# Half-row product groups in the opening of a fused Fourier-mixing and attention kernel, with 48 score-maximum tiles ahead and zero products before the first loads

## The chip, the cores and the metric

The kernel runs on one core of one Trainium2 chip. The metric is the device time of one execution in microseconds; the time before is the median of three runs. A profiled execution stands beside them; its trace gives all durations.

## The reference

```python
def reference(A_x, A_dft_seq_re, A_dft_seq_im, A_dft_hid_re, A_dft_hid_im, B_x, B_wqkv, B_wo, gate_w):
    x = A_x                                             # [1, 2048, 512], float32
    g = sigmoid((x * gate_w).sum(-1, keepdims=True))
    # Fourier mixing: hidden DFT, then sequence DFT, real part only
    re = x @ dft_hid_re.T
    im = x @ dft_hid_im.T
    a = dft_seq_re @ re - dft_seq_im @ im
    # attention: 32 heads of 16
    q, k, v = split_heads(x @ wqkv)
    b = merge_heads(softmax(q @ k.T * 16 ** -0.5) @ v) @ wo
    return g * a + (1 - g) * b
```

## The kernel before

Matrix products that need float32 accuracy are made from parts: a matrix is split into a high part in the reduced format `float32r` (a cast, `hi_lo`) and a low part (source minus high part), and a product is the sum of three: high by high, high by low, low by high (`mm3`). A chain over the hidden size of 512 therefore has 4 x 3 = 12 products of 128 rows by 512 columns into one PSUM bank. There are eight banks: `banks[0..6]` and `psD`.

The work goes in stages.

**Opening.** The inputs are loaded into a ring of six scratch tiles `raw` (`RAW`), split by ScalarE (high) and VectorE or GpSimd (low), and q and k are made for four blocks of 512 rows. q and k go to DRAM by their parts. The first product needs the first `wqkv` and `xa_t` blocks.

**v and imaginary rows.** For each of 16 blocks of 128 rows, a chain makes v (to the tile `vt`: ScalarE copies one half, VectorE the other); for each of 16 blocks another chain makes the imaginary part of the hidden DFT (`wch`, `wcl`), which ScalarE and VectorE split into a tile `hl` (two buffers) and SyncE's queue writes to DRAM (`b_d`). After `s` = 6, 8, 10, 12 a block of `wo` is split on ScalarE and GpSimd and a block of `w_hid` loaded; after the first four imaginary chains these become `wre`, the weights of the real part, whose low parts GpSimd makes. These chains take turns of three banks (`turn_of("s")`).

Between these chains, from the eighth on, stand *visits*: `visit(i)` makes two pairs of maximum tiles. A maximum tile (`a_tile`) is a product of 48 rows (16 rows of q and k, three combinations of parts) for one head, 128 queries and 512 keys; VectorE reduces it to the row maxima. A pair is the same tile for the two heads of a head pair, on rows 0 to 47 and 64 to 111. They take turns of four banks (`turn_of("a")`). `LEAD` = 44 pairs are made there, and `a_next` counts them. When the 32 pairs of one half of a head pair are done, `m_parts` (a reduction on VectorE, two small operations on GpSimd) and then `m_rows` (a transposition on VectorE, four small DMAs each on SyncE's and GpSimd's queues, `qs<-mt`) are queued in `deferred`; they put the negated maxima as two more rows beside q, so that the score product subtracts them. One entry is taken from `deferred` at each visit, or at the end of each segment later.

**Main stage.** From line 378 on, a `segment` interleaves on TensorE: half-row products (64 rows) of the real hidden DFT and the sequence DFT (`d`, into `psD`), beside a score or a maximum tile on the other half of the rows. ScalarE takes the exponential of each score tile (`pt`). A segment ends with 16 products of exponentials by v (`pv`). The patterns `FULL`, `THIN` and `NINE` fix the order; a segment has eight maximum tiles until their stream is used up, and the lead of this stream over the scores stays as the stage before left it. A planner (`bank`, `read_by`) picks the bank of each score and maximum tile by an estimate of when it is free. Loads and the final steps are due at fixed score units (`plan`). The second half of a `d` chain waits, by a dependency added by hand, for a reader of the segment before, so that both halves of the rows do not write one bank at the same time.

At the end of the sequence DFT `end_tiles` loads the output weights (`wo_hl`, four DMAs of 512 KB, line 462) and the attention rows over the no longer needed `xab` tiles, and the output projection follows.

Of the kernel before, what the change touches and what calls it, by code (L numbers as in the profile page):

```python
# [9 lines left out]
F32 = mybir.dt.float32  # L10
F32R = mybir.dt.float32r
AF = mybir.ActivationFunctionType
ALU = mybir.AluOpType
AX = mybir.AxisListType

P = 128
S = 2048
D = 512
# [3 lines left out]
KT = D // P  # L22
NT = S // P
UNITS = NP * 32
LEAD = 44
RAW = 6
PSUM = bass.MemoryType.PSUM
DRAM = bass.MemoryType.DRAM
# [3 lines left out]
def mix_kernel(ctx: ExitStack, tc: tile.TileContext, xa_t, xa, wqkv, w_hid, w_seq, wo, gate_w, out):  # L32
# [5 lines left out]
    nc = tc.nc  # L38
    ctx.enter_context(tc.manual_schedule())

    banks = [ctx.enter_context(tc.tile_pool(name=f"ps{i}", bufs=1, space=PSUM)) for i in range(7)]
    psD = ctx.enter_context(tc.tile_pool(name="psD", bufs=1, space=PSUM))
# [6 lines left out]
    b_d = [dram.tile([P, 2, D], F32, name=f"b{s}") for s in range(NT)]  # L49
# [22 lines left out]
    xab = [const.tile([P, 4, 2, D], F32R, name=f"xab{tb}", tag=f"xab{tb}") for tb in range(4)]  # L72

    turns = dict.fromkeys("fsa", 0)

    def turn_of(kind):

        group = {"f": range(7), "s": range(3), "a": range(3, 7)}[kind]
        turns[kind] += 1
        return banks[group[(turns[kind] - 1) % len(group)]].tile([P, 512], F32, name="t")  # L80

    def hi_lo(hi, lo, src, lo_eng=None):
        nc.scalar.copy(hi, src)  # L83
        (lo_eng or nc.vector).tensor_tensor(lo, src, hi.bitcast(F32), ALU.subtract)  # L84

    def mm3(ps, sh, sl, mh, ml, first, last):
        nc.tensor.matmul(ps, sh, mh, start=first, stop=False)  # L87
        nc.tensor.matmul(ps, sh, ml, start=False, stop=False)  # L88
        nc.tensor.matmul(ps, sl, mh, start=False, stop=last)  # L89

    right = tc.tile_pool(name="st1", bufs=1, side="right", reuse_waits="tile")
    st1 = right.__enter__()
    wv = [[const.tile([P, D], F32R, name=f"wv{v}{kt}", tag=f"w{4 * v + kt}") for kt in range(KT)] for v in range(2)]
    wch = st1.tile([P, KT, D], F32R, name="wch")
    wcl = st1.tile([P, KT, D], F32R, name="wcl")
# [10 lines left out]
    def add(hi, lo, src, lo_eng, shape=None):  # L106
        todo.append((hi, lo, src, lo_eng, shape))
# [6 lines left out]
    def split(n):  # L114

        for _ in range(n):
            load_ahead()
            if loaded:
                hi, lo, raw, lo_eng, shape = loaded.pop(0)
                hi_lo(hi, lo, raw.rearrange("p (s t) -> p s t", s=4) if shape else raw, lo_eng)  # L120
            load_ahead()

    def add_x(tb, kt):
        x = xab[tb][:, :, :, kt * P:(kt + 1) * P]
        add(x[:, :, 0], x[:, :, 1], xa_t[tb, :, kt], nc.vector, True)


    with tc.tile_pool(name="qk", bufs=1, reuse_waits="tile") as pool:
        wh = pool.tile([P, 2, KT, D], F32R, name="wh")
        wl = pool.tile([P, 2, KT, D], F32R, name="wl")  # L130

        def mm_qk(ps, c, ct, tb, kt):
            cols = slice(ct * P, (ct + 1) * P)
            x = xab[tb][:, :, :, kt * P:(kt + 1) * P]
            mm3(ps, wh[:, c, kt, cols], wl[:, c, kt, cols], x[:, :, 0], x[:, :, 1], kt == 0, kt == KT - 1)

        def evac_qk(ps, c, ct, tb):
            hl = pool.tile([P, 2, D], F32R, name="hl", bufs=7)
            hi_lo(hl[:, 0], hl[:, 1], ps)
            nc.sync.dma_start(qk_d[c][:, ct * P:(ct + 1) * P, tb * 512:(tb + 1) * 512].rearrange("v p t -> p v t"),  # L140
                              hl.bitcast(F32))

        for kt in range(KT):
            add(wh[:, 0, kt], wl[:, 0, kt], wqkv[0, :, kt], nc.vector)
            add_x(0, kt)
        for kt in range(KT):
            add(wh[:, 1, kt], wl[:, 1, kt], wqkv[1, :, kt], nc.vector)
        for tb in range(1, 4):
            for kt in range(KT):
                add_x(tb, kt)  # L150
        for kt in range(KT):
            add(wv[0][kt], wv[1][kt], wqkv[2, :, kt], nc.gpsimd)
        for kt in range(KT):
            add(wch[:, kt], wcl[:, kt], w_hid[1, :, kt], nc.gpsimd)
        split(8)

        xgs = {}

        def gate_row(s):

            xg = xgs.pop(s)
            nc.vector.scalar_tensor_tensor(xg, xg, 1.0, gwb, op0=ALU.mult, op1=ALU.mult, accum_out=z[:, s:s + 1])
            if s + 5 < NT:
                xgs[s + 5] = staged(xa[s + 5])

        for tb in range(4):
            if tb == 2:
                assert not todo and not loaded
                nc.sync.dma_start(gwb, gate_w.broadcast_to([P, D]))
                xgs.update({s: staged(xa[s]) for s in range(5)})  # L170
            for c in range(2):
                if tb == 0 and c == 0:
                    pss = [turn_of("f") for _ in range(4)]
                    for kt in range(KT):
                        for ct in range(4):
                            mm_qk(pss[ct], c, ct, tb, kt)
                    split(4)
                    for ct in range(4):
                        evac_qk(pss[ct], c, ct, tb)
                    continue  # L180
                for ct in range(4):
                    ps = turn_of("f")
                    for kt in range(KT):
                        mm_qk(ps, c, ct, tb, kt)
                    split(1 if ct % 2 and tb else 2)
                    evac_qk(ps, c, ct, tb)
                    if tb > 1:
                        gate_row(8 * (tb - 2) + 4 * c + ct)
# [19 lines left out]
    deferred = []  # L208
    a_left = {}

    def a_tile(i, h, ps=None):
        p, j = divmod(i, 64)
        qt, kb = divmod(j, 4)
        if ps is None:
            ps = turn_of("a")
        r = slice(64 * h, 64 * h + 48)
        nc.tensor.matmul(ps, qs[p % 2][r, qt * P:(qt + 1) * P], ks[p % 2][r, kb * 512:(kb + 1) * 512],  # L217
                         start=True, stop=True)
        user = nc.vector.tensor_reduce(mx[p % 2][:, h, qt, kb:kb + 1], ps, AX.X, ALU.max)  # L219
        hf = j // 32  # L220
        a_left[p, hf] = a_left.get((p, hf), 64) - 1
        if not a_left[p, hf]:
            deferred.extend((partial(m_parts, p, hf), partial(m_rows, p, hf)))
        return user
# [32 lines left out]
    wrs = []  # L257
    a_next = 0

    def visit(i):  # L260

        nonlocal a_next
        if deferred:
            deferred.pop(0)()
        if i < 7 or a_next == LEAD:
            return
        for j in range(2):
            for h in range(2):
                a_tile(a_next, h)
            a_next += 1  # L270

    for s in range(NT):
        t = xab[s // 4][:, s % 4]
        ps = turn_of("s")
        for kt in range(KT):
            r = slice(kt * P, (kt + 1) * P)
            mm3(ps, t[:, 0, r], t[:, 1, r], wv[0][kt], wv[1][kt], kt == 0, kt == KT - 1)
        visit(s)
        pv = ps.rearrange("p (r h d) -> p r h d", h=2, d=DH)
        nc.scalar.copy(vt[:, s, :, 0:16], pv[:, :, 0])  # L280
        nc.vector.tensor_copy(vt[:, s, :, 17:33], pv[:, :, 1])
        if s in range(6, 14, 2):
            kt = (s - 6) // 2
            wt = st1.tile([P, 2, D], F32R, name="hl", bufs=2)
            hi_lo(wt[:, 0], wt[:, 1], wos.pop(0), nc.gpsimd)
            nc.sync.dma_start(wo_d[kt], wt.bitcast(F32))
            wrs.append(staged(w_hid[0, :, kt]))

    def spare(i, dt, name):

        return const.tile([P, 4, P], dt, name=name, tag=f"w{i}")


    wre = [[const.tile([P, D], F32R, name=f"wre{v}{kt}", tag=f"w{4 * v + kt}") for kt in range(KT)] for v in range(2)]
    ab = [xab[s // 4][:, s % 4] for s in range(NT)]
    for s in range(NT):
        t = ab[s]
        ps = turn_of("s")
        for kt in range(KT):
            r = slice(kt * P, (kt + 1) * P)  # L300
            mm3(ps, t[:, 0, r], t[:, 1, r], wch[:, kt], wcl[:, kt], kt == 0, kt == KT - 1)
        visit(NT + s)
        bt = st1.tile([P, 2, D], F32R, name="hl", bufs=2)
        hi_lo(bt[:, 0], bt[:, 1], ps)
        nc.sync.dma_start(b_d[s], bt.bitcast(F32))
        if s < KT:
            hi_lo(wre[0][s], wre[1][s], wrs.pop(0), nc.gpsimd)
    run_deferred()
    assert a_next == LEAD
    right.__exit__(None, None, None)  # L310
# [516 lines left out]
    users, valued = [], 0  # L827
# [80 lines left out]
    users = []  # L908
# [68 lines left out]
```

## Time and profile before

| | |
|---|---|
| median of 3 runs | 1710.47 us (1710.4 to 1710.5) |
| profiled execution | 1713.87 us |
| its span, first to last instruction | 1712.1 us |
| mean granted TensorE clock | 0.997 |
| busy: TensorE / VectorE / ScalarE / GpSimd | 99% / 80% / 73% / 42% |

Times are from the start of the span. A timeline row gives the start, the time from there to the end of the row's last instruction, the engine, the line, the operation, output and inputs, the shape, the count, and in brackets the idle time before it with what ended it. PE is TensorE's products, PEld its weight loads, DVE VectorE, ACT ScalarE, POOL GpSimd, SPq SyncE's queue. A product's row is as long as its passage through the array; products follow each other more closely than that, so the start of one to the start of the next is its cost. A row of a group of instructions gives the busy time, the mean of one in ns, and the idle time before them.

### The profile page before, as it was taken

Reading aid. Unit: us, or ns where it says so; the run is one execution under the profiler, and the core shown is the slowest. Engines: PE = TensorE matmul, PEld = TensorE weight load, DVE = VectorE, ACT = ScalarE, POOL = GpSimd, SP = SyncE. Lnnn points to the kernel's source line nnn. Section 1 sums busy time; section 2 is a strip of 40 time slices with the busy share of each in tenths; the row PEclk is TensorE's granted clock in tenths of the full one; section 3 lists DMA queues with packets and bytes.
Section 4 is the critical chain, followed back from the end, with each engine's and each line's share of the span. In section 5 each row is a group of like instructions: output and inputs, shape, how many; then the busy total and the mean of one; then the engine's idle time right before and its main releaser. Section 6 shows DMA issues by size and latency. Waiting matters only on the chain.

```text
span 1712.1 us, 33831 instructions
## 1 busy us (share of the span) xinstructions
PE 1693.7 (99%) x12731; PEld 1081.6 (63%) x12731; DVE 1376.3 (80%) x2298; ACT 1247.9 (73%) x2472; POOL 715.4 (42%) x775
## 2 busy tenths in 40 slices
PE   8999999999999999999999999999999999999997
PEld 7876666666666666666666666666666656555543
DVE  5448788888888888888888888888888888799943
ACT  5212288887787788778788788778778778778785
POOL 0211144454444455444444555545455555322230
PEclk9999999999999999999999999999999999999999
DMA  8972511314141525232146635241322535560114
GB/s 280 341 173 98 159 16 19 46 32 81 53 80 46 95 89 103 60 67 59 40 92 247 125 94 108 57 87 51 72 73 66 106 100 101 183 151 8 39 27 136
DMA packets 82484, 165.12 MB, mean 96 GB/s; under 512 B 19776, under 2 KB 20032, under 8 KB 78480
## 3 DMA queue, kind: packets, MB, share of 16 engines
q1 hardware_dynamic: 77968, 162.56, 37.1%
q8 instruction: 100, 1.64, 0.4%
q0 software_dynamic: 4352, 0.39, 0.3%
q14 instruction: 64, 0.52, 0.1%
HBM read 107.73 MB, written 54.52 MB: 95 GB/s over the span
## 4 chain that ended last, share of the span: by engine, by line
PE 97%; DVE 1%; DMA 1%; issue 0%; POOL 0%; ACT 0%; SPq 0%; DVEq 0%; POOLq 0%; ACTq 0%
PE d L378 38%; PE t L718 27%; PE t L217 11%; PE t L682 9%; PE t L87 4%; PE t L88 3%; PE t L89 3%; PE t L699 1%; DVE mx L219 1%; PE t L378 0%; DMA qs<-mt 0%; DMA raw<-wqkv 0%; DVE yp L559 0%; PE t L637 0%; DMA o<-osum 0%
## 5 line engine op out<-in xcount | busy, mean ns | idle before, releaser
L219 DVE TENSOR_REDUCE mx<-t 128x1 f32<-128x512 f32 x2048 | 1267.4, 682 | 218.2 <-PE t L217 185.0
L683 ACT ACTIVATE pt<-t 128x512 f32<-128x512 f32 x2048 | 1034.9, 632 | 14.4 <-PE t L682 10.5
L682 PE MATMUL t<-qs,ks 50*128 50x512 f32 x2048 | 745.0, 414 | 3.6 <-DMA qs<-mt 2.4
L217 PE MATMUL t<-ks,qs 48*128 48x512 f32 x2048 | 695.5, 404 | 0.3 <-DVE mx L219 0.2
L378 PE MATMUL d<-xab,ch 64*128 64x512 f32 x2016 | 648.6, 396 | 0.0
L718 PE MATMUL t<-pt,vt 128*32 128x512 f32 x3968 | 478.9, 600 | 0.0
L378 PEld LDWEIGHTS d<-xab,ch 64*128 64x128 f32 x2016 | 367.1, 185 | 131.7 <-issue 90.7
L217 PEld LDWEIGHTS t<-ks,qs 48*128 48x128 f32 x2048 | 366.4, 186 | 79.0 <-DVE mx L219 26.3
L378 PE MATMUL d<-xab,cl 64*128 64x512 f32 x1008 | 399.4, 396 | 0.0
L682 PEld LDWEIGHTS t<-qs,ks 50*128 50x128 f32 x2048 | 367.6, 185 | 39.4 <-ACT pt L683 12.6
L733 POOL TENSOR_TENSOR osum<-osum,oe 128x512 f32<-128x512 f32 x217 | 278.9, 1285 | 124.4 <-ACT oe L727 118.5
L727 ACT COPY oe<-t 128x512 f32<-128x512 f32 x217 | 127.3, 587 | 254.1 <-PE t L718 252.5
L718 PEld LDWEIGHTS t<-pt,vt 128*32 128x32 f32 x3968 | 105.1, 109 | 230.2 <-issue 149.9
L333 POOL CAST ch<-craw 128x512 fp32r<-128x512 f32 x126 | 77.0, 611 | 377.9 <-PE t L682 364.5
L378 PEld LDWEIGHTS d<-xab,cl 64*128 64x128 f32 x1008 | 186.2, 185 | 67.5 <-issue 53.6
L334 POOL TENSOR_TENSOR cl<-craw,ch 128x512 fp32r<-128x512 f32 x126 | 162.1, 1286 | 10.2
L240 POOL DMA_DIRECT2D qs<-mt x128 | 72.0, 568 | 101.5 <-DVE mt L236 94.6
L83 ACT CAST hl<-t 128x512 fp32r<-128x512 f32 x48 | 28.1, 586 | 85.2 <-PE t L89 67.3
L378 PE MATMUL d<-wre,xab 64*128 64x512 f32 (+1 forms) x348 | 85.5, 391 | 0.1
L378 PE MATMUL d<-wo_hl,o_hl 64*128 64x512 f32 (+1 forms) x261 | 69.7, 393 | 0.0
L378 PEld LDWEIGHTS d<-wre,xab 64*128 64x128 f32 (+1 forms) x348 | 64.0, 185 | 7.0 <-issue 1.1
L84 DVE TENSOR_TENSOR hl<-t,hl 128x512 fp32r<-128x512 f32 x48 | 32.9, 687 | 37.6 <-ACT hl L83 37.6
(115 smaller groups left out, 890.8 us busy)
## 6 DMA issues: line engine op xcount, KB each, us to landing
craw<-w_seq SPq DMA_DIRECT2D x128, 256.0 KB
qk<-hl SPq DMA_DIRECT2D x32, 512.0 KB
qs<-qk SPq DMA_DIRECT2D x96, 128.0 KB
ks<-qk SPq DMA_DIRECT2D x96, 128.0 KB
b<-hl SPq DMA_DIRECT2D x16, 512.0 KB
xab<-b SPq DMA_DIRECT2D x16, 512.0 KB
o<-osum SPq DMA_DIRECT2D x62, 128.0 KB
oh<-nh SPq DMA_DIRECT2D x12, 512.0 KB
```

Of the source, the lines that this page charges most:

```text
L87: nc.tensor.matmul(ps, sh, mh, start=first, stop=False)
L217: nc.tensor.matmul(ps, qs[p % 2][r, qt * P:(qt + 1) * P], ks[p % 2][r, kb * 512:(kb + 1) * 512], start=True, stop=True)
L219: user = nc.vector.tensor_reduce(mx[p % 2][:, h, qt, kb:kb + 1], ps, AX.X, ALU.max)
L240: (nc.sync, nc.gpsimd)[h].dma_start(rows.rearrange("v (q b c) -> v b q c", q=8, b=4)[:, b], mt[hf][32 * b + h:32 * b + 32:2])
L333: nc.gpsimd.tensor_copy(h1, raw)
L334: nc.gpsimd.tensor_tensor(l1, raw, h1.bitcast(F32), ALU.subtract)
L378: i = nc.tensor.matmul(self.ps, st[r], mv[r], start=not self.begun, stop=stop)
L682: nc.tensor.matmul(ps, ks[p % 2][rr, kt * P:(kt + 1) * P], qs[p % 2][rr, q0:q0 + 512], start=True, stop=True)
L683: return nc.scalar.activation(pts[u][:, 2 * qb + h], ps, AF.Exp, bias=0.0, scale=DH ** -0.5)
L718: nc.tensor.matmul(acc[32 * j:32 * j + 32], vt[:, kt, p, h:h + 32], pt[:, j], start=u == us[0], stop=u == us[-1])
L727: nc.scalar.copy(oe, acc)
L733: nc.gpsimd.tensor_tensor(o, o, oe, ALU.add)
```

## The change

Three things are changed.

Eight products of a zeroed weight tile are put ahead of everything else on TensorE; VectorE writes the zeros.

The first eight v chains are as before, without visits. The other eight v chains and the sixteen imaginary chains go in groups of four (`four`), each with a bank of its own. A group has four phases. In phase 0 the first 64 rows of chain 0 and the last 64 rows of chain 1 alternate, in phase 1 those of chains 2 and 3; in phases 2 and 3 each chain gets the other half of its rows. Phases 2 and 3 begin with a dependency by hand on a reduction of maxima made in the phase before. In each phase two pairs of maximum tiles are made, after the fourth and the ninth product of each half: 24 phases by 2 are 48 pairs, the new `LEAD`. Chains take turns of four banks, maxima of three and `psD`.

The parts of the imaginary rows are made otherwise: ScalarE copies the bank to a `raw` tile, and GpSimd makes the high and the low part from it (`b_done`).

```diff
-LEAD = 44
+LEAD = 48
...
-        group = {"f": range(7), "s": range(3), "a": range(3, 7)}[kind]
+        group = {"f": banks, "s": banks[:4], "a": [*banks[4:], psD]}[kind]
...
+        nc.vector.memset(wch[:, 0].bitcast(F32), 0.0)
+        ps = turn_of("f")
+        for _ in range(8):
+            nc.tensor.matmul(ps, wch[:, 0, :P], wch[:, 0], start=True, stop=True)
         split(8)
...
-    def visit(i):
-
-        nonlocal a_next
-        if deferred:
-            deferred.pop(0)()
-        if i < 7 or a_next == LEAD:
-            return
-        for j in range(2):
-            for h in range(2):
-                a_tile(a_next, h)
-            a_next += 1
...
+    def row_products(s, wh, wl):
+
+        t = ab[s]
         for kt in range(KT):
-            r = slice(kt * P, (kt + 1) * P)
-            mm3(ps, t[:, 0, r], t[:, 1, r], wv[0][kt], wv[1][kt], kt == 0, kt == KT - 1)
-        visit(s)
+            hi, lo = (t[:, v, kt * P:(kt + 1) * P] for v in range(2))
+            yield from ((hi, wh[kt]), (hi, wl[kt]), (lo, wh[kt]))
...
-        visit(NT + s)
+    def b_done(s, ps):
+
+        raw = st1.tile([P, D], F32, name="raw", bufs=RAW)
+        nc.scalar.copy(raw, ps)
         bt = st1.tile([P, 2, D], F32R, name="hl", bufs=2)
-        hi_lo(bt[:, 0], bt[:, 1], ps)
+        nc.gpsimd.tensor_copy(bt[:, 0], raw)
+        nc.gpsimd.tensor_tensor(bt[:, 1], raw, bt[:, 0].bitcast(F32), ALU.subtract)
         nc.sync.dma_start(b_d[s], bt.bitcast(F32))
         if s < KT:
             hi_lo(wre[0][s], wre[1][s], wrs.pop(0), nc.gpsimd)
+
+    def maxima():
+
+        nonlocal a_next
+        users = [a_tile(a_next, h) for h in range(2)]
+        a_next += 1
+        return users[1]
+
+    def four(ss, wh, wl, done):
+
+        ps = [turn_of("s") for _ in ss]
+        seen = None
+        for phase, pair in enumerate(((0, 1), (2, 3), (1, 0), (3, 2))):
+            guard, seen = seen, None
+            both = [row_products(ss[c], wh, wl) for c in pair]
+            for j in range(12):
+                for half, c in enumerate(pair):
+                    st, mv = next(both[half])
+                    r = slice(64 * half, 64 * half + 64)
+                    i = nc.tensor.matmul(ps[c], st[r], mv[r], start=phase < 2 and j == 0, stop=phase > 1 and j == 11)
+                    if phase > 1 and j == 0:
+                        tc.add_manual_dep(
+                            i.ins, guard.ins.name,
+                            mybir.DependencyInfo(mybir.DependencyClass.Sync, mybir.DependencyReason.DATA))
+                if j in (3, 8):
+                    user = maxima()
+                    seen = seen or user
+            if deferred:
+                deferred.pop(0)()
+            if phase > 1:
+                for c in sorted(pair):
+                    done(ss[c], ps[c])
+
+    for s in range(8):
+        ps = turn_of("s")
+        products = list(row_products(s, *wv))
+        for j, (st, mv) in enumerate(products):
+            nc.tensor.matmul(ps, st, mv, start=j == 0, stop=j == 11)
+        v_done(s, ps)
+    for s in range(8, NT, 4):
+        four(range(s, s + 4), *wv, v_done)
...
+    for s in range(0, NT, 4):
+        four(range(s, s + 4), [wch[:, kt] for kt in range(KT)], [wcl[:, kt] for kt in range(KT)], b_done)
```

More of the change, by code (lines that the diff above doesn't have):

```diff
@@ L76, in turn_of @@
     def turn_of(kind):
-        group = {"f": range(7), "s": range(3), "a": range(3, 7)}[kind]
+        group = {"f": banks, "s": banks[:4], "a": [*banks[4:], psD]}[kind]
         turns[kind] += 1
-        return banks[group[(turns[kind] - 1) % len(group)]].tile([P, 512], F32, name="t")
+        pool = group[(turns[kind] - 1) % len(group)]
+        return pool.tile([P, 512], F32, name="d" if pool is psD else "t")
     def hi_lo(hi, lo, src, lo_eng=None):
@@ L258, in mix_kernel, with v_done @@
     a_next = 0
-    def visit(i):
-        nonlocal a_next
-        if deferred:
-            deferred.pop(0)()
-        if i < 7 or a_next == LEAD:
-            return
-        for j in range(2):
-            for h in range(2):
-                a_tile(a_next, h)
-            a_next += 1
-    for s in range(NT):
-        t = xab[s // 4][:, s % 4]
-        ps = turn_of("s")
+    ab = [xab[s // 4][:, s % 4] for s in range(NT)]
+    def row_products(s, wh, wl):
+        t = ab[s]
         for kt in range(KT):
-            r = slice(kt * P, (kt + 1) * P)
-            mm3(ps, t[:, 0, r], t[:, 1, r], wv[0][kt], wv[1][kt], kt == 0, kt == KT - 1)
-        visit(s)
+            hi, lo = (t[:, v, kt * P:(kt + 1) * P] for v in range(2))
+            yield from ((hi, wh[kt]), (hi, wl[kt]), (lo, wh[kt]))
+    def v_done(s, ps):
         pv = ps.rearrange("p (r h d) -> p r h d", h=2, d=DH)
@@ L287, in mix_kernel @@
             wrs.append(staged(w_hid[0, :, kt]))
+    def b_done(s, ps):
+        raw = st1.tile([P, D], F32, name="raw", bufs=RAW)
+        nc.scalar.copy(raw, ps)
+        bt = st1.tile([P, 2, D], F32R, name="hl", bufs=2)
+        nc.gpsimd.tensor_copy(bt[:, 0], raw)
+        nc.gpsimd.tensor_tensor(bt[:, 1], raw, bt[:, 0].bitcast(F32), ALU.subtract)
+        nc.sync.dma_start(b_d[s], bt.bitcast(F32))
+        if s < KT:
+            hi_lo(wre[0][s], wre[1][s], wrs.pop(0), nc.gpsimd)
+    def maxima():
[34 more added lines that the diff above has]
+        four(range(s, s + 4), *wv, v_done)
     def spare(i, dt, name):
@@ L294, in mix_kernel @@
     wre = [[const.tile([P, D], F32R, name=f"wre{v}{kt}", tag=f"w{4 * v + kt}") for kt in range(KT)] for v in range(2)]
[L295 to L301, printed above, removed]
-        visit(NT + s)
-        bt = st1.tile([P, 2, D], F32R, name="hl", bufs=2)
-        hi_lo(bt[:, 0], bt[:, 1], ps)
-        nc.sync.dma_start(b_d[s], bt.bitcast(F32))
-        if s < KT:
-            hi_lo(wre[0][s], wre[1][s], wrs.pop(0), nc.gpsimd)
+    for s in range(0, NT, 4):
+        four(range(s, s + 4), [wch[:, kt] for kt in range(KT)], [wcl[:, kt] for kt in range(KT)], b_done)
     run_deferred()
```

## The prediction

> **What bounds the kernel now.** I read the page's totals and its chain first.
>
> ```profile
> PE 1693.7 (99%) x12731; PEld 1081.6 (63%) x12731; DVE 1376.3 (80%) x2298; ACT 1247.9 (73%) x2472; POOL 715.4 (42%) x775
> PE 97%; DVE 1%; DMA 1%; issue 0%; POOL 0%; ACT 0%; SPq 0%; DVEq 0%; POOLq 0%; ACTq 0%
> ```
>
> TensorE is the path from end to end, so an edit pays only if it shortens the row of matmul starts, or closes a hole in it. The change touches three places: the first 12 us, the stretch of v and imaginary chains, and (through `LEAD`) the order of everything after. I took each from the timeline, and the second also from the busy time by window.
>
> ```profile
> 95.86:203.31 107.45, 107.45 (x474) 77.00 (x473) 71.27 (x124) 19.74 (x40) 17.95 (x23) 1.00 0.45 133
> 95.86 0.39 PE L87 MATMUL t<-wv,xab 128*128 128x512 f32 x1
> 98.58 0.39 PE L87 MATMUL t<-wv,xab 128*128 128x512 f32 x1
> 143.00 0.73 PE L217 MATMUL t<-ks,qs 48*128 48x512 f32 x4
> 143.66 0.50 PE L87 MATMUL t<-wv,xab 128*128 128x512 f32 x1
> 146.62 0.73 PE L217 MATMUL t<-ks,qs 48*128 48x512 f32 x4
> 203.31 1.53 PE L378 MATMUL d<-wre,xab 128*128 128x512 f32 x6
> ```
>
> The first row is a window (its length; busy time and count of TensorE, weight loads, VectorE, ScalarE, GpSimd; granted clock; DMA share; GB/s), from the first v product to the first real product: 107.45 us, TensorE never idle, clock full. A chain of 12 products on all 128 rows takes 98.58 - 95.86 = 2.72 us, 0.227 a product. With a visit (four 48-row products for row maxima) the period is 146.62 - 143.00 = 3.62. So 32 chains are 87.0 us, and the remaining 20.4 belong to 22 visits, 0.93 each: two pairs of 48-row products that run two at a time would need 0.46, and the rest is lost in changing from 128-row to 64-row products and back.
>
> ```profile
> 699.82 0.39 PE L378 MATMUL d<-xab,ch 64*128 64x512 f32 x1
> 699.83 0.39 PE L217 MATMUL t<-ks,qs 48*128 48x512 f32 x1
> 702.10 0.39 PE L378 MATMUL d<-xab,ch 64*128 64x512 f32 x1
> 702.19 0.39 PE L682 MATMUL t<-qs,ks 50*128 50x512 f32 x1
> ```
>
> This is the main stage, where every product has 64 rows or fewer and works beside one on the other half. From 699.82 to 702.10 lie ten such slots: 0.228 us a slot, two products in each, with no change of form.
>
> **1. Half-row groups: -9.1 us.** Eight v chains stay whole: 8 x 2.72 = 21.8. The other 24 chains become six groups of four phases, each phase 12 slots of products and 2 slots of maxima: 24 x 14 = 336 slots at 0.228 = 76.6. Together 98.4 against 107.45, and four more pairs of maxima (48 for 44) are inside it. A visit's 0.93 becomes two slots, 0.46; that is the whole gain, since two half products in a slot do the work of one whole product.
>
> Does anything else end later than TensorE in a phase of 14 x 0.228 = 3.19 us?
>
> ```profile
> 194.15 0.73 PE L217 MATMUL t<-ks,qs 48*128 48x512 f32 x4
> 194.68 2.48 DVE L219 TENSOR_REDUCE mx<-t 128x1 f32<-128x512 f32 x4 [0.58 <-PE t L217]
> L83 ACT CAST hl<-t 128x512 fp32r<-128x512 f32 x48 | 28.1, 586 | 85.2 <-PE t L89 67.3 <-DMA b<-hl 4.6 <-DVE nm L228 3.1
> L84 POOL TENSOR_TENSOR wre<-raw,wre 128x512 fp32r<-128x512 f32 x4 | 5.2, 1292 | 20.5 <-ACT wre L83 20.5
> L395 POOL CAST xab<-y 128x512 fp32r<-128x512 f32 x12 | 7.3, 610 | 89.9 <-ACT y L394 61.6 <-PE t L217 28.3
> ```
>
> Four reductions take 2.48 us, so one each 0.60 in a row; a phase's four need 2.4 of 3.19, and the vector engine no longer makes the low parts of the imaginary rows. The new guard (phases 2 and 3 wait for a reduction of the phase before, with all of TensorE's queue behind it) asks for the second reduction of a pair issued at slot 4: 0.91 + 0.53 (194.15 to 194.68) + 0.60 + 0.68 = 2.7 us, before the phase ends at 3.19. I cost the guard at nothing; the vector engine hides it, with 0.5 us to spare, and if it lagged by more, each of 12 guards would pay the lag.
>
> Not nothing are two places. **First imaginary group, +1.6.** Each row's high and low part now come from GpSimd: 0.61 + 1.29 = 1.90 us. For the first four rows GpSimd also makes a low part of `wre` (1.29), in the order row, wre, row, wre. The scratch ring `raw` has six buffers; counted through, the fourth row's copy out of PSUM takes the buffer of the second `w_hid` block, which is free only when that block's low part is made. From the end of phase 2: product end and copy 1.05, then 2 x 1.90 + 2 x 1.29 = 6.4, then the copy 0.59: bank free at 8.0. The next group's phase 1 wants that bank after two phases, 6.4. TensorE waits 1.6 us. **Entry to the main stage, +1.0.** The last maxima now sit in the real chains' bank `psD`; its reduction ends 2.28 + 0.53 + 0.60 + 0.68 = 4.1 us after the phase began, against 3.19. Both could be 0 (a ring or queue a little ahead) or double (GpSimd's spans are rough): 0 to +5 together.
>
> In steady state GpSimd has 1.90 a chain of 3.19. Its two `hl` buffers wait for the row's DMA:
>
> ```profile
> 198.53 0.69 DVE L84 TENSOR_TENSOR hl<-t,hl 128x512 fp32r<-128x512 f32 x1 [0.76 <-ACT hl L83]
> 203.70 0.59 ACT L83 CAST hl<-t 128x512 fp32r<-128x512 f32 x1 [1.98 <-DMA b<-hl]
> ```
>
> A buffer full at 198.53 + 0.69 = 199.22 was free at 203.70, 4.5 us later. One buffer then turns in 1.90 + 4.5 = 6.4 us for two chains, whose phases take 6.4: just enough, and six `raw` buffers absorb a small lag.
>
> **2. Zero products: -1.6 us.**
>
> ```profile
> 1.35 0.23 DVE L62 TENSOR_TENSOR pairsum<-ident 128x64 f32<-128x64 f32 x1 [1.35 <-POOL ident masks.py:199]
> 5.72 0.80 PE L87 MATMUL t<-xab,wh 128*128 128x512 f32 x1 [5.72 <-ACT xab L83]
> 10.88 0.63 PE L89 MATMUL t<-xab,wl 128*128 128x512 f32 x1
> 11.31 0.58 PE L87 MATMUL t<-xab,wh 128*128 128x512 f32 x1
> 11.72 0.39 PE L88 MATMUL t<-xab,wh 128*128 128x512 f32 x1
> 11.95 0.40 PE L89 MATMUL t<-xab,wl 128*128 128x512 f32 x1
> ```
>
> Products start every 0.43 us up to 11.3 and every 0.23 from 11.7: the fast pace came 6.0 us after the first product. The zero tile is written behind `pairsum`; no vector memset stands in the trace, so I take 0.6 us (the 0.69 of a row-sized vector operation as the upper bound, 0.2 as the lower). Eight products from 2.3 us at 0.43 end at 5.7, where the first real one starts anyway. If the pace follows the start of the stream, it comes 3.4 us earlier, and the products made in that time cost 0.23 for 0.43: 3.4 x (1 - 0.227/0.427) = 1.6. Bounds: 0, if zeros do not count, to 6.0 x 0.47 = 2.8, if the pace is there with the first real product.
>
> **3. Lead 48: -5.8 and -0.5 us.** A segment has eight maxima, and a segment is 5.82 us; four pairs more are one segment. So each pair's row values (`m_rows`) are sent one segment earlier against the scores that need them. In one place that matters:
>
> ```profile
> 1453.45 0.50 PE L378 MATMUL d<-xab,ch 64*128 64x512 f32 x1
> 1459.27 0.50 PE L378 MATMUL d<-xab,ch 64*128 64x512 f32 x1
> 1462.31 2.54 SPq L462 DMA_DIRECT2D wo_hl<-wo  x4
> 1463.99 0.56 POOL L240 DMA_DIRECT2D qs<-mt  x1 [2.63 <-issue]
> 1465.10 0.50 PE L378 MATMUL d<-xab,ch 64*128 64x512 f32 x1
> 1469.64 0.76 PE L682 MATMUL t<-qs,ks 50*128 50x512 f32 x1 [2.43 <-DMA qs<-mt]
> 1476.70 0.49 PE L378 MATMUL d<-xab,ch 64*128 64x512 f32 x1
> 1465.00:1470.00 5.00, 2.57 (x21) 1.89 (x19) 2.02 (x4) 2.56 (x5) 3.95 (x4) 0.92 0.98 344
> 1470.00:1475.00 5.00, 5.00 (x25) 3.02 (x27) 3.26 (x5) 2.39 (x4) 0.00 (x0) 0.50 0.05 17
> 1660.00:1680.00 20.00, 18.95 (x117) 7.82 (x115) 7.67 (x11) 16.22 (x33) 1.13 (x1) 1.00 0.41 97
> ```
>
> A normal segment is 1459.27 - 1453.45 = 5.82; the one from 1465.10 takes 11.60. A score waited 2.43 us for the last row values, issued late (1463.99) into the burst of `wo_hl` loads (344 GB/s), and then the clock was granted at 0.50. One segment earlier these values leave before 1462.31, and the score's place does not move: wait and half clock go, -5.8. Next late would be the segment's own 5.82.
>
> The other effect is where the maxima's stream ends:
>
> ```profile
> 1610.72 1.93 PE L718 MATMUL t<-pt,vt 128*32 128x512 f32 x16
> 1616.67 1.92 PE L718 MATMUL t<-pt,vt 128*32 128x512 f32 x16
> 1633.92 1.92 PE L718 MATMUL t<-pt,vt 128*32 128x512 f32 x16
> 1638.98 2.61 PE L718 MATMUL t<-pt,vt 128*32 128x512 f32 x16
> ```
>
> Two segments of one pattern: 5.95 with eight reductions, 5.06 in the last, which has four. After the change the last has none and the one before it four. Their floor is 12 slots and the value products, 12 x 0.228 + 1.92 = 4.66, so the last can gain 0.4 and the other about as much: -0.5 (0 to -1).
>
> [...]
>
> **Sum.** -9.1 + 1.6 + 1.0 - 1.6 - 5.8 - 0.5 = -14.4. The profiled execution took 1713.87 us (span 1712.1 and 1.8 around), so 1699.5; it stands 3.4 above the median of 1710.47. The sum carried over gives **1696.1**. About 3.4 us (0.2%) is what can be told from no change.
>
> **Rivals.** (a) *The late row values are no part of the gain*: the timed runs are shorter than the profiled one by 3.4 and may not have this hole, or the earlier values meet another burst. For it: it is one event in one execution. Against: the loads that delay it are in every run. Then -8.6: 1701.9. (b) *The clock drops after the new wait*, +3.4: 1699.5; or zeros buy nothing, +1.6: 1697.7. (c) *GpSimd becomes the bound of the imaginary groups*: if a row's write takes 6 us, not 4.5, a buffer turns in 7.9 against 6.4 and 16 chains lose 8 x 1.5 = 12, less some 4 (an estimate: two of the six buffers ahead, at 1.90 each) that `raw` absorbs: 1704. For it: the equality above. (d) *Slower: two 64-row chains do not share a slot as a chain and a score do.* In the visit the four maxima took 143.66 - 143.00 = 0.66 for two slots, 0.33 each. At 0.33, 336 slots cost 34 more: 1730. It decides from 0.228 + 14.4/336 = 0.271 a slot. Against it stands the main stage, 64 rows beside 50 at 0.228; for it, that no trace shows 64 beside 64.
>
> **How the numbers follow.** Forecast 0.58; (a) 0.19; (b) 0.09; (c) 0.06; (d) 0.05; 0.03 that gains and waits cancel. The low end is the sum with the new waits at nothing and the pace at 2.8, 1696.1 - 2.6 - 1.2 = 1692, less 1 for the tail: 1691. The high end reaches past (a) with no gain from zeros, 1703.5, and (c), 1704: 1705. Faster (below 1707.0): forecast, (a), (b) and two thirds of (c), 0.90; same 0.03; slower: (d) and the rest of (c), where the waits also drop the clock, 0.07.
>
> **What would show it.** Right: the stretch from the first v product to the first real one 101 us; a hole of 1 to 2 us once, at phase 1 of the second imaginary group, waiting for ScalarE's copy, that for GpSimd; products 0.23 apart from about 8.3 us; no wait for `qs<-mt`, all full segments at 5.82. Wrong: slots over 0.25 in the groups, vector reductions as releaser of TensorE at each phase's start, half clock inside the groups, or the score still waiting at the `wo_hl` loads.

## The result, and the profile after

| | before | after |
|---|---|---|
| median of the timed runs | 1710.49 us (1710.4 to 1710.8) | 1700.66 us (1699.7 to 1702.7, 4 runs) |
| profiled execution | 1713.87 us | 1699.70 us |
| its span | 1712.08 us | 1697.59 us |

The ratio is 0.9944, with a 95% interval of 0.9932 to 0.9956: faster, by 9.8 us in the median and by 14.2 in the profiled executions. That these two differ by a third is the main lesson of the case.

Totals, chain, and the window from the first v product to the first real one:

```profile
PE 1684.1 (99%) x13027; PEld 1084.1 (64%) x13027; DVE 1368.3 (81%) x2283; ACT 1246.5 (73%) x2472; POOL 746.2 (44%) x807
PE 98%; DVE 1%; ACT 0%; DMA 0%; POOL 0%; issue 0%; SPq 0%; DVEq 0%; POOLq 0%; ACTq 0%
93.61:194.60 100.99, 100.31 (x770) 81.04 (x768) 68.97 (x117) 18.63 (x41) 43.21 (x51) 1.00 0.47 132
115.46:141.38 25.92, 25.92 (x225) 21.20 (x226) 21.63 (x38) 4.52 (x11) 5.16 (x4) 1.00 0.32 103
141.38:194.60 53.22, 52.54 (x451) 42.00 (x447) 43.07 (x70) 10.82 (x22) 33.15 (x38) 1.00 0.36 138
```

TensorE is still the path. The stretch fell from 107.45 to 100.99 us. It is idle for 100.99 - 100.31 = 0.68 us, all at its end. The last two rows split it at the first half-row product and the first imaginary one: 25.92 / 112 = 0.231 us a slot in the v groups and, without the idle 0.68, 52.54 / 224 = 0.235 in the imaginary ones.

The timeline at the entry to the real rows, then the scratch copies of the first imaginary group:

```profile
193.86 0.68 DVE L224 TENSOR_REDUCE mx<-d 128x1 f32<-128x512 f32 x1
194.60 1.66 PE L416 MATMUL d<-wre,xab 128*128 128x512 f32 x6 [0.68 <-DVE mx L224]
...
154.76 0.59 ACT L289 COPY raw<-t 128x512 f32<-128x512 f32 x1 [1.20 <-PE t L315]
155.24 0.62 ACT L84 CAST wre<-raw 128x512 fp32r<-128x512 f32 x1
155.28 0.61 POOL L291 CAST hl<-raw 128x512 fp32r<-128x512 f32 x1
155.76 0.59 ACT L289 COPY raw<-t 128x512 f32<-128x512 f32 x1
157.22 1.28 POOL L85 TENSOR_TENSOR wre<-raw,wre 128x512 fp32r<-128x512 f32 x1
```

The first real product waits for the reduction of a maximum in `d`, which is bank `psD`: the entry wait is there. The wait for the scratch ring is not: the fourth row's copy stands at 155.76, directly behind the cast before it, while the low part of the second `w_hid` block comes only at 157.22.

The timeline of the start, and of the place where the kernel before had its hole:

```profile
2.16 3.78 PE L159 MATMUL t<-wch 128*128 128x512 f32 x8 [2.16 <-DVE wch L156]
5.79 0.79 PE L88 MATMUL t<-xab,wh 128*128 128x512 f32 x1
6.97 0.40 PE L90 MATMUL t<-xab,wl 128*128 128x512 f32 x1
7.21 0.40 PE L88 MATMUL t<-xab,wh 128*128 128x512 f32 x1
...
1450.92 0.50 PE L416 MATMUL d<-xab,ch 64*128 64x512 f32 x1
1451.47 0.56 POOL L245 DMA_DIRECT2D qs<-mt  x1 [0.76 <-issue]
1453.96 2.60 SPq L500 DMA_DIRECT2D wo_hl<-wo  x4
1456.75 0.50 PE L416 MATMUL d<-xab,ch 64*128 64x512 f32 x1
1462.57 0.49 PE L416 MATMUL d<-xab,ch 64*128 64x512 f32 x1
1468.68 0.50 PE L416 MATMUL d<-xab,cl 64*128 64x512 f32 x1
```

Products are 0.23 apart from 6.97 us, where it was 11.72. The last of the four transfers of row values leaves 2.5 us before the `wo_hl` loads, and the two segments that took 17.43 us take 1456.75 - 1450.92 = 5.83 and 1462.57 - 1456.75 = 5.82. The next takes 6.11. Segments of 6.09 to 6.11 stand at four places after and at none before; 1.1 us together.

The tail, by the starts of the value products, with two rows of the kernel before ahead:

```profile
1628.58 1.92 PE L718 MATMUL t<-pt,vt 128*32 128x512 f32 x16
1646.18 1.92 PE L718 MATMUL t<-pt,vt 128*32 128x512 f32 x16
...
1608.25 1.92 PE L756 MATMUL t<-pt,vt 128*32 128x512 f32 x16
1614.79 1.92 PE L756 MATMUL t<-pt,vt 128*32 128x512 f32 x16
1619.24 1.92 PE L756 MATMUL t<-pt,vt 128*32 128x512 f32 x16
1623.82 1.92 PE L756 MATMUL t<-pt,vt 128*32 128x512 f32 x14
1631.50 1.92 PE L756 MATMUL t<-pt,vt 128*32 128x512 f32 x16
```

The last three are 4.45, 4.58 and 7.68 us, together 16.71; the same three were 5.34, 5.06 and 7.20, together 1646.18 - 1628.58 = 17.60. That is 0.9 less.

### The profile page after: what moved, and what is told of

Same layout as the page of the kernel before. It is cut to its first block, busy times and chain, and to the rows that moved or that the text cites. A ratio compares the mean times of both kernels' runs of the same rounds, so it can differ in the third digit from the quotient of the medians.

```text
span 1697.6 us, 34437 instructions
## 1 busy us (share of the span) xinstructions
PE 1684.1 (99%) x13027; PEld 1084.1 (64%) x13027; DVE 1368.3 (81%) x2283; ACT 1246.5 (73%) x2472; POOL 746.2 (44%) x807
## 4 chain that ended last, share of the span: by engine, by line
PE 98%; DVE 1%; ACT 0%; DMA 0%; POOL 0%; issue 0%; SPq 0%; DVEq 0%; POOLq 0%; ACTq 0%
PE d L416 40%; PE t L756 27%; PE t L222 11%; PE t L720 9%; PE t L315 4%; PE t L88 2%; PE t L89 2%; PE t L90 2%; PE t L333 1%; PE t L737 1%; DVE mx L224 1%; PE t L416 0%; ACT pt L721 0%; PE t L159 0%; DVE yp L597 0%; PE t L675 0%
## 5 line engine op out<-in xcount | busy, mean ns | idle before, releaser
L416 PEld LDWEIGHTS d<-wo_hl,o_hl 64*128 64x128 f32 (+1 forms) x261 | 47.9, 185 | 4.4 <-issue 0.6
L88 PE MATMUL t<-xab,wh 128*128 128x512 f32 x128 | 50.2, 392 | 0.0
```

The costliest lines, as they stand in the source:

```text
L416: i = nc.tensor.matmul(self.ps, st[r], mv[r], start=not self.begun, stop=stop)
```

## The experiments

Each set ran beside the kernel before on one chip, another chip for each set; so a difference between two sets is less sure than one within a set. The kernel before had medians of 1711.29 (1709.5 to 1714.4, 27 runs), 1711.99 (1708.9 to 1713.8, 13 runs) and 1711.32 (1708.4 to 1713.8, 11 runs).

### Set 1: the parts one by one

**Zero products alone**, in the kernel before:

```diff
+        nc.vector.memset(wch[:, 0].bitcast(F32), 0.0)
+        ps = turn_of("f")
+        for _ in range(8):
+            nc.tensor.matmul(ps, wch[:, 0, :P], wch[:, 0], start=True, stop=True)
```

> The kernel before with the eight zero products alone. Theory (the fast pace starts with the stream of products, not with the first real one): the first v product starts 2.2 us earlier than before (95.86 to about 93.6), the median falls by 2.2 to 1708.3. [...] The hole at the wo_hl loads should be as in the kernel before, 2.4 us and a half clock, if it belongs to every execution of that order.

1711.39 us (1708.5 to 1712.1), ratio 0.9997 (0.9988 to 1.0006). In its trace the first v product is at 93.98, 1.9 us earlier. The hole is still there, and looks different:

```profile
1461.07 2.54 SPq L466 DMA_DIRECT2D wo_hl<-wo  x4
1462.70 0.56 POOL L244 DMA_DIRECT2D qs<-mt  x1 [2.64 <-issue]
1468.77 0.59 PE L686 MATMUL t<-qs,ks 50*128 50x512 f32 x1 [2.84 <-DMA qs<-mt]
1465.00:1470.00 5.00, 2.16 (x15) 1.61 (x13) 1.75 (x4) 2.16 (x5) 2.75 (x3) 0.90 0.78 256
1470.00:1475.00 5.00, 5.00 (x33) 2.78 (x31) 3.08 (x5) 2.17 (x4) 0.00 (x0) 0.76 0.00 2
```

The wait is longer than before (2.84 for 2.43) and the half clock shorter: if the granted clock was either 1.00 or 0.50, between which it changes in the kernel before, 0.90 and 0.76 over 5 us mean 1.0 + 2.4 = 3.4 us. Before, the rows gave 0.92 and 0.50, and the next one, of the kernel before:

```profile
1475.00:1480.00 5.00, 5.00 (x41) 3.27 (x33) 2.51 (x5) 3.10 (x7) 1.30 (x1) 0.90 0.12 13
```

0.8 + 5.0 + 1.0 = 6.8 us. So the hole is not one fixed price. The trace agrees with the theory, the median does not: it is 0.1 above the 1711.29 of the kernel before in this set. But the interval reaches from 2.1 us faster to 1.0 us slower, so this run does not decide whether timed runs have the 1.9 us of the trace.

**48 pairs ahead alone**, in the kernel before (`LEAD = 48` in 24 visits):

> The kernel before with 48 pairs ahead in place of 44, made in two more visits. Theory (the row values sent a segment earlier close the hole in every execution): two visits cost 2 x 0.93 = 1.9 us, the hole gives 5.8, the end of the maxima's stream 0.9: median 1705.7. Rival (the hole is in the profiled execution alone, or is only partly in the timed ones): no wait for the row values in the trace either, but the median at 1710.5 + 1.9 - 0.9 = 1711.5.

1708.00 us, ratio 0.9979 (0.9970 to 0.9988), and all 11 runs lie within 1707.5 to 1708.4. That is between the theory's 1705.7 and the rival's 1711.5. The row values leave before the loads, the segments are even, and the tail is 0.9 shorter:

```profile
1460.80 0.56 POOL L240 DMA_DIRECT2D qs<-mt  x1 [0.75 <-issue]
1463.25 1.25 SPq L462 DMA_DIRECT2D wo_hl<-wo  x2
94.90:204.29 109.39, 109.39 (x481) 77.54 (x480) 76.03 (x132) 19.74 (x40) 17.98 (x23) 1.00 0.45 130
```

The two more visits cost 109.39 - 107.45 = 1.9 us. With 0.9 back in the tail, the closed hole was worth 3.3 + 1.9 - 0.9 = 4.3 us in the timed runs, where the profiled execution shows 5.8.

**`wo_hl` loads later**, in the kernel before:

```diff
-            end_tiles(s // 4)
+            if s // 4 == 1:
+                end_tiles(0)
+            if s // 4:
+                end_tiles(s // 4)
```

> The kernel before with the four loads of wo_hl issued one step later in the last chain of the sequence DFT (with the first load of attention rows). Theory (the last row values were late because they ran into these loads): no wait for qs<-mt in the trace at the end of the sequence DFT, profiled time 5.8 us shorter; the median shorter by what of the hole the timed runs have, 1704.7 if all. Rival (the row values are late for another reason, the order on GpSimd's queue): the 2.4 us wait stays, median 1710.5.

1711.45 us (1709.5 to 1714.4), ratio 1.0003: a miss, because the edit did not do what it was for. SyncE issued the loads at 1462.28, where it was 1462.31: the later place in the program had nothing on SyncE's queue between it and the old one. The score waited 3.17 us. It says nothing on the theory.

**The changed kernel without the zero products:**

> The changed kernel without the zero products. Theory: the first v product is 2.2 us later than in the changed kernel (93.6 to 95.9), everything after it unchanged: median 1700.7 + 2.2 = 1702.9. Rival (later loads and queues take up the earlier start): median within 0.5 of the changed kernel's 1700.7.

1701.02 us (1700.6 to 1701.7), ratio 0.9941 (0.9928 to 0.9953). Its first v product is at 95.89, 2.3 us later than with zeros. The changed kernel wasn't in this set. Against its first median, 1700.66, this is the rival's case (within 0.5); against the one of set 2 below it is 1.5 us. So these runs do not settle what the zeros bring.

### Set 2: the hole and the entry

**The changed kernel again:**

> The changed kernel as it is, beside its variants: about 1700.7 us, within 1 us from run to run if the late row values no longer wait for the loads of wo_hl; runs 2 us or more apart would say that another event still varies.

1699.48 us (1699.4 to 1700.4), ratio 0.9929 (0.9917 to 0.9942).

**The loads behind another wait.** The experiment that failed, mended: the first `wo_hl` load is issued behind the load of the second block's tiles, which waits for a later release. The 44 pairs stay.

```diff
-            end_tiles(s // 4)
+            if s // 4:
+                end_tiles(s // 4)
+            if s // 4 == 1:
+                end_tiles(0)
```

> The kernel before with its 44 pairs, the loads of wo_hl issued behind the load of the second block's tiles on SyncE's queue, which waits for a later release: so they start some 10 us later. Theory (the burst delays the row values): these land in about 2 us, the score waits under 0.5 us, both segments are 5.82, and the timed runs come to about 1708.4 in place of 1711.3, within 1 us from run to run. Rival: GpSimd's own wait of 2.6 us ahead of the last of the four transfers is there without the burst too; then the score still waits 0.5 us or more and the time stays above 1710. If the loads delay what needs wo_hl in the output stage, a new wait shows there.

1707.59 us (1706.8 to 1708.7), ratio 0.9977 (0.9967 to 0.9987).

```profile
1463.54 0.56 POOL L240 DMA_DIRECT2D qs<-mt  x1 [2.63 <-issue]
1464.64 0.49 PE L378 MATMUL d<-xab,ch 64*128 64x512 f32 x1
1470.44 0.50 PE L378 MATMUL d<-xab,ch 64*128 64x512 f32 x1
1473.42 2.77 SPq L465 DMA_DIRECT2D wo_hl<-wo  x4
```

GpSimd's wait of 2.63 us is still there, but the transfer now lands 1.7 us after its issue, not 5.5, and the segment is 1470.44 - 1464.64 = 5.80, where it was 11.60. The burst makes the hole; GpSimd's wait only brings the transfer into it. The gain, 4.4 us, agrees with the 4.3 above.

**The changed kernel with 44 pairs ahead** (in the last group's four phases the second pair is left out):

```diff
-LEAD = 48
+LEAD = 44
...
-                if j in (3, 8):
+                if j == 3 or j == 8 and (done is v_done or ss[0] < NT - 4):
```

> The changed kernel with 44 pairs of maxima ahead: the second pair is left out in the last group's four phases. Theory (the row values sent one segment later meet the burst of wo_hl loads, and how long a score waits for them varies from execution to execution): in the trace the score waits 2 to 3 us for qs<-mt at about 1455 us and the clock is granted at half after it, the last segments are 0.9 us longer, and the timed runs are some 3.3 us over the changed kernel's (what 48 pairs brought the kernel before: 1711.3 to 1708.0) and spread over 4 us. Rival: the groups alone moved the loads or the scores so that they no longer meet; then it is at most 1 us over, with a narrow spread.

1702.43 us (1700.7 to 1705.2), 2.95 over the changed kernel, where 3.3 was expected. The runs lie 4.5 us apart, but that is the work of one run; the version with `psD` first, below, has such a run too, without the hole.

```profile
1452.64 2.54 SPq L500 DMA_DIRECT2D wo_hl<-wo  x4
1454.31 0.56 POOL L245 DMA_DIRECT2D qs<-mt  x1 [2.64 <-issue]
1459.73 0.47 PE L720 MATMUL t<-qs,ks 50*128 50x512 f32 x1 [2.21 <-DMA qs<-mt]
1460.00:1465.00 5.00, 5.00 (x43) 2.92 (x42) 3.46 (x6) 3.00 (x6) 0.00 (x0) 1.00 0.09 35
93.93:193.19 99.26, 99.26 (x761) 80.27 (x759) 63.92 (x109) 18.07 (x39) 42.23 (x50) 1.00 0.46 133
```

The score waits as foretold, 2.21 us; the half clock that I also foretold did not come (1.00 behind it). The stretch is 1.7 us shorter than with 48 pairs, the four slots and the entry wait, which I had not counted.

**`psD` first among the maxima's banks**, in the changed kernel:

```diff
-        group = {"f": banks, "s": banks[:4], "a": [*banks[4:], psD]}[kind]
+        group = {"f": banks, "s": banks[:4], "a": [psD, *banks[4:]]}[kind]
```

> The changed kernel with the maxima's three PSUM tiles handed out in the order psD, 5, 6 in place of 5, 6, psD, so that the last of the 48 maxima are not in the tile that the first real chain takes. Theory (the 1.06 us between products at the start of the real rows is a slot of 0.23 and 0.84 us of waiting for VectorE's last reductions in psD): the gap shrinks to a slot and the time is 0.8 us less than the changed kernel's. Rival: VectorE is as late for the next tile as it was for psD, the wait moves by a chain, and the time is the same.

```profile
93.31:193.56 100.25, 100.25 (x770) 81.06 (x768) 68.28 (x116) 18.07 (x39) 42.51 (x50) 1.00 0.46 132
```

The maxima have four banks, not the three that the expectation counts. TensorE is never idle in the stretch, which is 0.74 us shorter: the entry wait is gone, as expected of the bank's order. The timed runs don't confirm a gain: 1699.82 us (1698.4 to 1703.6) against 1699.48.

### Set 3: the groups, GpSimd, and a better version

**The groups alone** (44 pairs, no zeros):

> The groups alone: the changed kernel with 44 pairs of maxima ahead and without the zero products. Theory (336 half-row slots at 0.23 us in place of visits of 0.93): the stretch from the first v product to the first real one is 8 us shorter than the kernel before's (99.3 for 107.45), the late row values meet the wo_hl loads as before, and the timed runs are 7.5 to 9 us under the kernel before's, with a spread of some 4 us. Rival (part of the gain of the 44-pair version came from the zero products): 6 us or less.

1701.64 us (1700.9 to 1702.5), ratio 0.9943 (0.9932 to 0.9955): 9.7 under the kernel before, a little over the theory's 9, and with a spread of 1.6 us where 4 was expected. Its stretch is the 99.26 us of the 44-pair version of set 2, 8.2 less. The rest may be the hole: in this trace the score waits only 1.38 us for the row values, with no half clock (1.00 in the rows behind it), so the groups seem to have moved the two streams against each other too. That the timed runs have the same is not shown.

**ScalarE and VectorE make the imaginary rows' parts**, as before, in the changed kernel:

```diff
-        raw = st1.tile([P, D], F32, name="raw", bufs=RAW)
-        nc.scalar.copy(raw, ps)
...
-        nc.gpsimd.tensor_copy(bt[:, 0], raw)
-        nc.gpsimd.tensor_tensor(bt[:, 1], raw, bt[:, 0].bitcast(F32), ALU.subtract)
+        hi_lo(bt[:, 0], bt[:, 1], ps)
```

> The changed kernel with the imaginary rows' two parts made by ScalarE and VectorE from PSUM, as in the kernel before, in place of ScalarE's copy and GpSimd. Theory (no wait of the groups ended on GpSimd or on the raw copies, so who makes the parts doesn't matter): the stretch from the first v product to the first real one stays at 101.0 us, and the time is that of the changed kernel within 0.7 us. Rival 1 (GpSimd's work slows the slots of the imaginary groups, 0.233 against 0.231 of the v groups): 0.5 us or more faster. Rival 2 (VectorE has no room for 16 further subtractions of 0.69 us between the reductions that the phases wait for): waits on VectorE's maxima at the phases' starts, up to 11 us slower.

1701.47 us (1700.9 to 1704.2), ratio 0.9944 (0.9932 to 0.9956). The stretch, and one place where its weight loads wait:

```profile
93.31:197.34 104.03, 102.79 (x770) 81.19 (x768) 76.53 (x131) 18.78 (x40) 17.96 (x23) 1.00 0.46 136
157.85 0.18 PEld L312 LDWEIGHTS t<-wch,xab 64*128 64x128 f32 x1 [0.44 <-DVE hl L85]
159.04 0.18 PEld L222 LDWEIGHTS t<-ks,qs 48*128 48x128 f32 x1 [0.41 <-DVE mx L224]
```

104.03 - 100.99 = 3.0 us longer, through waits on VectorE: the second rival's mechanism, at a quarter of its price. My theory, that it doesn't matter who makes the parts, falls. In the same trace the segments of 6.1 us are gone, which gives 1.1 back; the net of 1.9 us is about what the timed runs show against the changed kernel's 1699.48 of set 2 (2.0).

**`psD` first and the loads later, both, with and without zeros:**

> The changed kernel with psD first among the maxima's tiles and the wo_hl loads behind those of the second block's tiles: it has neither the wait at the start of the real rows nor any burst near late row values. Expected 0.8 us under the changed kernel, about 1699 us, with no score waiting for row values. Rival: the variation left in the changed kernel does not come from the loads; then the runs still lie up to 5 us apart.

> The same without the zero products: what they bring where no hole blurs it. Theory (the full clock comes 3.4 to 5 us earlier behind zeros, as in the traces): the first v product is 2.2 us later in the trace and the timed runs 2.2 us longer. Rival (timed runs start with the clock already granted, or something else starts them): within 0.5 us of the version with zeros in the timed runs, although the trace shows 2.2.

With zeros 1698.30 us (1698.2 to 1699.5), ratio 0.9926 (0.9914 to 0.9937); without 1699.37 (1699.4 to 1700.9), ratio 0.9933 (0.9921 to 0.9944). So zeros bring 1.07 us here, between theory (2.2) and rival (under 0.5); the ranges touch and the intervals overlap, so the gain is likely and not shown. The two traces differ by 1.56 at the first v product (93.25 and 94.81); the one without zeros reached the pace of 0.23 us a product early, at 9.78 us. With zeros it is the fastest version, 1.2 us under the changed kernel's median of set 2, but the intervals of their ratios overlap.

## Why the prediction was right, and where it was wrong

The direction is right and the median lies in the range, 4.6 us above the forecast. The forecast of the profiled execution, 1699.5, was met (1699.7), in part by luck, since errors cancelled. By the steps:

| step | predicted | in the traces | in the timed runs |
|---|---|---|---|
| half-row groups | -9.1 | 100.25 - 107.45 = -7.2 | |
| scratch ring | +1.6 | 0 | |
| entry wait | +1.0 | +0.7 | |
| zeros | -1.6 | -2.3 (this pair) | -1.1 |
| hole | -5.8 | -5.8 | -4.3, -4.4 |
| tail | -0.5 | -0.9 | |
| segments of 6.1 us | none | +1.1 | |
| sum | -14.4 | -14.4 (spans: -14.5) | |

**Groups.** Two 64-row chains do share a slot, so rival (d) falls: 0.231 and 0.235 us, against 0.271 where it would decide. But I took 0.228 from inside a segment of the main stage. The 336 slots took 25.92 + 52.54 = 78.5 us against 336 x 0.228 = 76.6: the term was mis-sized by 1.9 us.

**Scratch ring: the step that failed.** I counted `raw` through as a ring of six and put the fourth copy in the buffer of the second `w_hid` block. The copy's row shows no wait for that block's low part, so its buffer was another one. By the same count the third copy would have waited for the first block's low part, which ends at 154.04 + 1.29 = 155.33 us; it starts at 154.76. How a pool hands out buffers has to be read from the instructions, not counted.

**GpSimd and VectorE.** The guards cost nothing, as I said, and rival (c) falls: TensorE waits nowhere in the stretch for GpSimd. The version with VectorE's parts shows how close the 0.5 us of room was: sixteen subtractions more, and TensorE waits 3.0 us.

**Zeros.** In the seven traces without zeros the first v product stands at 94.81 to 95.89, mean 95.4; in the seven with zeros at 93.25 to 93.98, mean 93.5. The mean gain of 1.9 is near my 1.6; the one pair of a single set without the hole says 1.1 in the timed runs. My mechanism, that the fast pace follows the start of the stream, holds roughly, not exactly: without zeros it begins 4.3 to 6.3 us after the first product, with zeros 4.5 to 6.1 us after the first zero product. The first v product follows the start of that pace: it stands at 93.61 us where the pace starts at 6.97 (the changed kernel), 93.98 for 8.26 (zeros alone), 94.81 for 9.78 and 95.86 for 11.72 (the kernel before). So what zeros bring differs from run to run by a us or more. What the traces show here is a pace, which the last expectation calls the full clock: in the kernel before the granted clock reads 1.00 from 5.72 to 11.72 us, with products 0.43 apart after the first ones, as it does from 11.72 on, with 0.23.

**Tail.** It gained 0.9 for my 0.5. Two segments now take 4.45 and 4.58 us, under the floor of 4.66 that I had added up.

**The hole, and the carry to the median: the other step that failed.** The mechanism is shown three ways: earlier row values close it, later loads close it, and 44 pairs bring it back. But I took its 5.8 us from one execution and carried the whole sum over to a median that lay 3.4 below that execution. Most likely the 3.4 was the hole, though no trace shows those three timed runs. It varies from run to run: the wait was 1.38 to 3.17 us in the five traces that have it and the half clock behind it 0, 3.4 or 6.8 us. In the three sets the versions with the hole spread by 1.6 to 5.4 us in the timed runs, 48 pairs in the kernel before by 0.9; the first four runs of the kernel before, with the hole, lie within 0.4. (Single runs 3 us above the rest are left in three versions without the hole; they are not explained.) An estimate from these: if the first three runs had a hole of 5.8 - 3.4 = 2.4, the sum of the right hand column and the traces is -7.2 + 0.7 - 1.1 - 2.4 - 0.9 + 1.1 = -9.8, which is what was measured. With the 4.3 of set 1 in place of 2.4 it would be -11.7, so how much of the hole those runs had stays an assumption. Rival (a) had priced this: without the hole it gave 1701.9, 1.2 above the result. I gave it 0.19 on the ground that the loads are in every run; they are, but not the same meeting of loads and row values.

**The clock behind the hole.** Gaps of 2.43, 2.84 and 3.17 us in TensorE's row were followed by half clock, for 6.8, 3.4 and 6.8 us by the rows of 5 us (the kernel before, zeros alone, the loads' line moved); gaps of 2.21 and 1.38 us (the changed kernel with 44 pairs, the groups alone) were not. No limit on the age of a gap fits both: in the kernel before the clock fell when the gap was 1469.20 - (1469.64 - 2.43) = 1.99 us old, and the gap of 2.21 us passed at 1.00. The rows at that fall, and the stretch of half clock:

```profile
1469.10:1469.20 0.10, 0.00 (x0) 0.00 (x0) 0.00 (x0) 0.00 (x0) 0.01 (x1) 0.98 0.92 348
1469.20:1469.30 0.10, 0.00 (x0) 0.00 (x0) 0.00 (x0) 0.00 (x0) 0.00 (x0) 0.50 0.94 369
1469.20:1476.03 6.83, 6.39 (x29) 3.60 (x33) 3.26 (x5) 2.39 (x4) 0.00 (x0) 0.50 0.12 46
```

In the same trace 20 us with 1.05 us idle (1660 to 1680, 18.95 busy) kept 1.00. What decides whether the clock falls is not shown. The forecast priced the new waits without a fall; the 3.4 us that rival (b) adds for one is what the hole of the kernel before cost beyond its wait, 11.60 - 5.82 - 2.43. No fall came: the wait for the scratch ring stayed away, and behind the entry wait of 0.68 us the clock is 1.00 (194.60 to 200.00).

**Open.** Why the segments of 6.1 us come. ScalarE's timeline in the segment of 5.82 and in the one of 6.11 behind it, in the changed kernel:

```profile
1456.94 0.59 ACT L765 COPY oe<-t 128x512 f32<-128x512 f32 x1 [1.31 <-PE t L756]
1457.42 4.03 ACT L721 ACTIVATE pt<-t 128x512 f32<-128x512 f32 x8
1463.06 0.59 ACT L765 COPY oe<-t 128x512 f32<-128x512 f32 x1 [1.60 <-PE t L756]
1463.54 4.04 ACT L721 ACTIVATE pt<-t 128x512 f32<-128x512 f32 x8
```

The copy of attention sums stands 1.60 us idle in place of 1.31, and the exponentials behind it are as much later. Such segments stand in all eight traces in which GpSimd makes the imaginary parts and in none of the other six; what holds the copy wasn't tried.

## What to carry to other kernels

Before a term is taken from a hole in one profiled execution, ask whether the hole lies in every run: if the median is below the profiled time, the difference may be that very hole, and carrying the sum over then counts it twice. Small transfers that something waits for should leave before a burst of large loads or the loads behind a later release (here the landing fell from 5.5 to 1.7 us); moving the loads' line in the program does nothing if nothing on the queue holds them (1462.28 us for 1462.31). Half-row chains in pairs save, by my estimate, the change of form between whole and partial products, here 7 of 107 us, as long as the engine that frees the banks keeps its room (with VectorE's sixteen subtractions more the stretch was 3.0 us longer).

## What I had not expected of the hardware

The fourth transfer of one set of row values, the 120th small transfer on GpSimd's queue, has an idle time in front of it that ends on nothing visible: 2.63 to 2.65 us in the six traces with 44 pairs ahead and 0.73 to 0.76 in the eight with 48. It stayed, at 2.63 us, when the loads were moved away, so they don't cause it; its cause is open. Its landing took 1.7 to 2.3 us where the loads were not under way and 4.4 to 6.2 us where they were.
